# Power tables with the exponent innermost, and the backward state-space and dW2 placed beside the last block's transforms

## The chip, the cores and the metric

The kernel runs on one core of one Trainium2 chip. The metric is the time of one execution on the device in microseconds; three executions of the kernel before gave 1028.64, 1029.13 and 1033.02 us, the median is 1029.13. A core has five engines with a queue of instructions each, served in order: PE (matrix products and transposes; PEld is its loading of weights), DVE (elementwise work), ACT (activation functions and copies), POOL and SP (here SP issues nearly all DMAs). [...]

## The reference

The program computes a forward pass and all gradients of it. With x of shape [2048, 512] and xn its layer norm without scale, s a long convolution whose kernel comes from a diagonal complex state space of 128 states for each of 512 channels, and an FFN with 1792 hidden units:

```python
    dt = exp(log_dt)[:, None];  logdA = dt * (A_re + 1j*A_im);  dB = dt * (B_re + 1j*B_im)
    P = exp(logdA[:, :, None] * l[None, None, :])            # l = 0 .. 2047
    K = einsum("dn,dnl,dn->dl", C_re + 1j*C_im, P, dB).real
    s = irfft(rfft(xn, padded) * rfft(K, padded)) + xn * Dskip
    g = silu(silu(xn @ w1) @ w2)
    out = x + s * g
```

Returned are `out` and the gradients with respect to x, the six state-space matrices, log_dt, Dskip, w1 and w2, for a given `grad_out`, all in bf16.

## The kernel before, in words

**Layout.** The 2048 positions are kept as 128 partitions by 16; the 512 channels are cut into four blocks of 128 (b = 0 to 3), the hidden units into 14 tiles of 128 (`ft`).

**Power tables.** The state-space kernel K needs exp(logdA * l) for l up to 2047. A power is put together as a product of a low and a high factor; the factors are tables of 64 channels ("a half", eight in all, built in turn into one buffer `T4`). `half_angles` (L448) multiplies lam by 24 exponents into `PC` (magnitudes `MG`, cosines and sines `RC`, f32) and takes Exp and Sin on ACT; `half_tables` (L466) multiplies magnitudes and cosines into the bf16 tables. `PC` is laid out as [3, 24 exponents, 64 channels], so the channel is innermost in all that is read and written there; the tables `vXL` and `vYL` (L471, L473) are laid out with the exponent innermost in memory and are viewed here with the channel innermost, so that the 448-element multiplies of L484 and L486 write every eighth bf16 element. `vXH` (L490) writes runs of fourteen. L495 to L501 make the factors Fc and G (f32, 3 exponents); ACT copies them into `vYH`.

**Forward state-space** (`gen_ssm_fwd`, a generator of 106 steps): per group of channels DVE multiplies table factors into `X` and `ym`, PE transposes them (the results go to DRAM as `xt_d` and `yt_d` for the backward pass) and sums K, which goes to `K_b` of its block.

**Convolution.** `gen_conv_y(b)` (30 steps) transforms xn and K of one block (`dft_fwd`: two sets of products with a set of transposes between them), multiplies (`cplx_mul`, on DVE) and transforms back (`dft_inv`) to s; it also makes DO, the gradient at the FFN's output, and the output block. `gen_conv_rest(b)` (29 steps) transforms the gradient ds and gives the gradient of xn (`DXC`) and of K (`dKs`), with two inverse transforms. Every product of these lands in PSUM and is evacuated by `k.ev`, an `Evac` object (L63): `Evac(nc, 0)` gives all copies to ACT, `Evac(nc, 2)` (`k.ev2`) every second one to DVE.

**Backward.** `gen_ffn_bwd`, three steps for each `ft`: the hidden activations `a_ft` and `th_ft` are loaded, `turn` transposes `a_ft` (16 transposes on PE, two evacuations); `da` = 16 products with W2T and DOT; DVE makes `dhT`; dW2 = 16 products of the turned activations with `DO_all`; then `dhT` is turned and dW1 = 16 products with xn, turned and stored. `gen_ssm_bwd(b)` (25 steps): for eight groups of channels products `psV` (8 matmuls) with `Gbd` (made from dKs), evacuation to `Vb`, multiplies with `YT` on DVE, and sums `psS` (8 matmuls). `gen_ssm_final`, for blocks 0 to 2 and then for block 3, turns the sums into gradients on DVE with many small DMAs. `gen_dx`: 16 groups of 14 products with dhT and W1T, then the layer norm's gradient on DVE and ACT.

**Order.** The program is written as generators whose steps are merged by `interleave` with weights. Order by hand, L206 to L245: FFN forward beside 42 steps of the forward state-space; y and rest of blocks 0 and 1 beside 26 steps each; y of block 2 beside the last 12; then, alone, y of block 3 (in a second set of buffers, `C3`), rest of block 2, `load_bwd` (W2T, DO_all and DOT by DMA, the first and last transposing), rest of block 3; then FFN backward beside 110 steps of backward state-space and finals, one to three; then dx. The framework lays each engine's instructions out in about this order; an instruction that by its own estimate isn't ready lets later, ready ones pass, and it inserts all waits.

**Memory.** Pools are stacks from the left and from the right of a partition's memory, the right one ending at byte 229344; constants fill the left up to byte 37024. A pool opened where another was waits, tile by tile, for the last user of what lay there.

Of the kernel before, what the change touches and what calls it, by code (L numbers as in the profile page):

```python
# [14 lines left out]
P = 128  # L15
# [12 lines left out]
T = 16  # L28
# [123 lines left out]
def kernel(ctx, tc, A_u, A_A_re, A_A_im, A_B_re, A_B_im, A_C_re, A_C_im, A_log_dt, A_Dskip, B_x, B_w1, B_w2, grad_out,  # L152
# [35 lines left out]
    k.ev = Evac(nc, 0); k.ev2 = Evac(nc, 2)  # L188

    st_l = ExitStack(); st_tf = ExitStack()  # L190
    k.tfp = st_tf.enter_context(pool("tf", "left"))
# [9 lines left out]
    k.K_b = {}  # L201
    gs = gen_ssm_fwd(k)
# [6 lines left out]
    st_c = ExitStack(); st_c3 = ExitStack(); st_f = ExitStack()  # L209
# [9 lines left out]

    C3 = KCtx(); C3.big = st_c3.enter_context(pool("cbig3", "left")); C3.io = st_c3.enter_context(pool("cio3", "left"))  # L220
    run(gen_conv_y(k, C3, NB - 1))
    run(gen_conv_rest(k, C, NB - 2))
    st_c.close()
    k.e1 = ctx.enter_context(pool("keep", "right"))
    k.fb = st_f.enter_context(pool("ffnb", "right"))
    load_bwd(k)
    run(gen_conv_rest(k, C3, NB - 1))
    st_c3.close(); st_tf.close()
    dhp = ctx.enter_context(pool("dhT", "left"))
    k.dhT = dhp.tile([P, k.FT, L], BF16, name="dhT")  # L230
    def state():
        with pool("ssmb", "left", 2) as k.bp:
            k.Gbd = k.bp.tile([P, 2, 2, 32, 64], BF16, name="Gbd", bufs=1)
            for e in range(2):
                nc.gpsimd.memset(k.Gbd[64 * e:64 * e + 64, :, 1 - e], 0.0)
            for b in range(NB):
                yield from gen_ssm_bwd(k, b)
# [4 lines left out]
    interleave([gen_ffn_bwd(k), BoundedGen(gst, 110)], [1, 3])  # L242
# [205 lines left out]
def half_angles(k, w0):  # L448
# [6 lines left out]
    sh = [P, 2, 24, 64]  # L455
    tmul(nc, PC[:, 0:3:2], k.lam[:, 0:2, ws].unsqueeze(2).to_broadcast(sh), k.ecst[:].rearrange("p (a m) -> p a m", a=2).unsqueeze(3).to_broadcast(sh))
# [5 lines left out]
    nc.scalar.activation(out=RC[:, 1, 0:10], in_=RC[:, 1, 0:10], func=ACT.Sin, scale=2.0 * math.pi)  # L462
    nc.scalar.activation(out=RC[:, 1, 10:24], in_=RC[:, 1, 10:24], func=ACT.Sin, scale=-2.0 * math.pi)


def half_tables(k, w0):  # L466
# [4 lines left out]
    vXL = T4[:, OXL:OXH].rearrange("p (c r l) -> p c l r", c=3, l=8)  # L471
    vXH = T4[:, OXH:OYL].rearrange("p (c r l u) -> p c r l u", c=2, l=8, u=2)
    vYL = T4[:, OYL:OYH].rearrange("p (c g y r l) -> p c l g y r", c=2, y=2, r=4, l=8)  # L473
    vYH = T4[:, OYH:HSZ].rearrange("p (c g y r m u) -> p c g y r m u", c=2, y=2, r=4, m=4, u=2)
    if w0 == 0:
        for c in range(3):
            nc.gpsimd.memset(vXL[:, c, 0], 1.0 if c == 0 else 0.0)
        for c in range(2):
            v = 1.0 - c
            nc.gpsimd.memset(vXH[:, c, :, 0, :], v)  # L480
            nc.gpsimd.memset(vYL[:, c, 0, :, 0, :], v)
            nc.gpsimd.memset(vYH[:, c, :, 0, :, 0, :], v)
    for c in range(2):
# [3 lines left out]
    nc.vector.tensor_scalar(out=T4[:, OXL + 1024:OXH], in0=T4[:, OXL + 512:OXL + 1024], scalar1=-1.0, scalar2=None, op0=ALU.mult)  # L487
    for c in range(2):
        hh = lambda t: t[:, 17:24].rearrange("p m r -> p r m").unsqueeze(3).to_broadcast([P, 64, 7, 2])
        tmul(nc, vXH[:, c, :, 1:8, :], hh(MG), hh(RC[:, c]))  # L490
    yl = T4[:, OYL:OYH].rearrange("p (a y r) -> p a y r", y=2, r=32)
    nc.vector.tensor_copy(out=yl[:, :, 1], in_=yl[:, :, 0])
    sh = [P, 2, 3, 64]
    Fc = RC[:, :, 7:10]
    tmul(nc, Fc, MG[:, 7:10].unsqueeze(1).to_broadcast(sh), Fc)  # L495
# [441 lines left out]
```

## Time and profile before

| | us |
|---|---|
| median of three executions | 1029.13 |
| profiled execution | 1028.81 |
| its span, first to last instruction | 1027.0 |
| PE, DVE, ACT busy in it | 761.4, 746.6, 649.1 |

A row of the profile's groups gives line, engine, operation, the tile written and those read, the shapes, the count, then the busy time in us and the mean of one in ns, and what ended the idle time before. L60, L72 and L74 are helpers (`tmul`, the two copies of `Evac`), so their groups are told apart by tile names. In rows of the timeline the first number is the start in us from the span's begin, the second the length.

### The profile page before, as it was taken

What the parts mean: (1) busy time and instruction counts of PE and PEld (TensorE: products, weight loads), DVE (VectorE), ACT (ScalarE), POOL (GpSimd) and SP (SyncE); (2) the same over time, 40 slices, a digit from 0 to 9 for tenths busy, and PEclk for the clock granted to TensorE, in tenths of its full rate; (3) what the DMA queues carried; (4) which work ended last, traced back from release to release, by engine and by line L of the source; (5) the groups of instructions that cost most, each with busy time, mean ns of one, the idle gap of its engine ahead of it and who ended that gap; (6) DMA issues with size and microseconds to landing.
All of it is one profiled execution on the core that took longest, in us unless ns stands there. A gap on an engine that the chain in (4) does not pass through costs nothing. (4 is left out here: it accounts for less than half of the span.)

```text
span 1027.0 us, 17231 instructions
## 1 busy us (share of the span) xinstructions
PE 761.4 (74%) x6809; PEld 480.1 (47%) x6809; DVE 746.6 (73%) x1191; ACT 649.1 (63%) x1122; POOL 21.3 (2%) x86
## 2 busy tenths in 40 slices
PE   0276868888766667666777677699889998996693
PEld 0144545454646556465655455444445444443241
DVE  6997979899789995899805363646567755586497
ACT  1677696988969878697777777544545553442022
POOL 3100000000000000000000002000000000000000
PEclk9778989999988978889888888899999999999897
DMA  5054465746754444253759119976688877648771
GB/s 118 12 193 154 165 190 170 201 153 201 175 54 119 109 103 63 41 137 97 122 108 81 15 42 212 245 200 215 172 259 232 244 182 222 202 130 108 82 139 50
DMA packets 218034, 146.76 MB, mean 143 GB/s; under 512 B 155424, under 2 KB 187552, under 8 KB 217952
## 3 DMA queue, kind: packets, MB, share of 16 engines
q1 hardware_dynamic: 216608, 139.89, 56.4%
q0 software_dynamic: 768, 3.67, 1.0%
q10 hardware_dynamic: 576, 2.10, 0.6%
q8 instruction: 53, 0.87, 0.4%
q14 instruction: 29, 0.24, 0.1%
HBM read 74.84 MB, written 62.13 MB: 133 GB/s over the span
## 5 line engine op out<-in xcount | busy, mean ns | idle before, releaser
L540 PE MATMUL pf_t<-ident_bfloat_78,X 128*128 128x128 bf16 x1024 | 79.4, 232 | 46.6 <-ACT th L601 12.2
L74 ACT CAST Vb<-psV 128x512 bf16<-128x512 f32 x128 | 66.9, 603 | 69.6 <-issue 45.5
L514 DVE TENSOR_TENSOR ym<-T_512 128x1024 bf16<-128x1024 bf16 x128 | 83.3, 690 | 27.8 <-PE pf_y L557 26.2
L540 PEld LDWEIGHTS <-X 128*128 128x128 bf16 x1024 | 69.2, 105 | 56.3 <-issue 38.9
L514 DVE TENSOR_TENSOR X<-T_512 128x1024 bf16<-128x1024 bf16 x128 | 81.8, 690 | 9.9 <-remote 5.8
L60 DVE TENSOR_TENSOR T_512<-PC 128x448 bf16<-128x448 f32 (+1 forms) x48 | 84.0, 1872 | 0.4 <-ACT PC L461 0.4
L74 ACT CAST XTf<-pf_t 128x512 bf16<-128x512 f32 x128 | 66.9, 631 | 0.3 <-PE pf_t L540 0.3
L611 PE MATMUL ps_o<-W_412,aT 128*128 128x512 bf16 x224 | 55.6, 405 | 12.4 <-ACT th_1502 L615 6.6
L769 PE MATMUL ps_dx<-W1T,dhT 128*128 128x512 bf16 x224 | 53.3, 404 | 14.3 <-DVE dxn L772 8.9
L597 PE MATMUL ps_h<-XNT,W_410 128*128 128x512 bf16 x224 | 55.3, 392 | 7.6 <-ACT th L601 7.6
L74 ACT COPY dftB<-pt_b 128x1024 bf16<-128x1024 bf16 x48 | 46.9, 1026 | 14.5 <-remote 7.3
L726 PE MATMUL ps_da<-DOT,W2T 128*128 128x512 bf16 x224 | 53.4, 379 | 0.2 <-ACT dKs L74 0.2
L808 PE MATMUL psV<-XT,Gbd 128*128 128x256 bf16 x256 | 39.5, 284 | 8.9 <-DMA XT<-xt_d 5.7
L95 PE MATMUL pt_b<-ident_bfloat_78,dftA 128*128 128x128 bf16 x384 | 35.3, 254 | 12.2 <-ACT dftA L74 8.4
L769 PEld LDWEIGHTS <-dhT 128*128 128x128 bf16 x224 | 23.0, 103 | 44.3 <-issue 21.0
L808 PEld LDWEIGHTS <-Gbd 128*128 128x128 bf16 x256 | 32.5, 176 | 19.9 <-issue 15.6
L739 PEld LDWEIGHTS <-DH 128*128 128x128 bf16 x224 | 20.1, 98 | 45.3 <-ACT DH L74 19.0
L611 PEld LDWEIGHTS <-aT 128*128 128x128 bf16 x224 | 22.5, 103 | 39.5 <-issue 19.1
L87 PEld LDWEIGHTS <-TF 128*128 128x128 bf16 x384 | 28.4, 108 | 25.0 <-issue 24.1
L778 ACT ACTIVATE lw<-xn,mm 128x512 f32<-128x512 bf16 x16 | 13.0, 813 | 42.8 <-DVE mm L775 40.6
L727 DVE SCALAR_TENSOR_TENSOR dhT<-th_ft,ps_da 128x512 bf16<-128x512 bf16 x56 | 35.6, 680 | 5.7 <-PE ps_da L726 5.5
L557 PE MATMUL pf_y<-ident_bfloat_78,ym 128*128 128x128 bf16 x384 | 38.9, 234 | 0.2
(1477 smaller groups left out, 1952.7 us busy)
## 6 DMA issues: line engine op xcount, KB each, us to landing
xt_d<-XTf SPq DMA_DIRECT2D x32, 512.0 KB, 2.9
XT<-xt_d SPq DMA_DIRECT2D x32, 512.0 KB, 4.6
YT<-yt_d SPq DMA_DIRECT2D x64, 256.0 KB, 4.1
yt_d<-YTf SPq DMA_DIRECT2D x32, 256.0 KB, 2.1
th_d<-th SPq DMA_DIRECT2D x28, 256.0 KB, 2.3
at_d<-aT SPq DMA_DIRECT2D x4, 1792.0 KB, 6.8
a_ft<-at_d SPq DMA_DIRECT2D x14, 512.0 KB, 4.8
th_ft<-th_d SPq DMA_DIRECT2D x14, 512.0 KB, 5.7
```

The source lines that it names most:

```text
L60: nc.vector.tensor_tensor(out=out, in0=a, in1=b, op=ALU.mult)
L74: self.nc.scalar.copy(out=out, in_=in_)
L95: nc.tensor.transpose(out=pt[:, gi, :], in_=A[:, c, g0 + gi, :, :].rearrange("p t e -> p (t e)"), identity=k.ident[:])
L514: nc.vector.tensor_tensor(out=out.rearrange("p (r h l u) -> p r h l u", h=nh, l=4, u=2), in0=h, in1=l, op=ALU.mult)
L540: nc.tensor.matmul(out=pf[:, qi, m // 2, :], lhsT=X[:, m, q + qi], rhs=k.ident[:], start=(m % 2 == 0), stop=(m % 2 == 1))
L557: nc.tensor.matmul(out=pt[:, Qi, m // 2, :], lhsT=ms[m][:, Q + Qi, 0], rhs=(k.nident if m == 1 else k.ident)[:], start=(m % 2 == 0), stop= ...
L597: nc.tensor.matmul(out=ps[:], lhsT=W1[:, dk, ft * P:(ft + 1) * P], rhs=XNT[:, dk, 4 * tcn:4 * tcn + 4, :], start=(dk == 0), stop=(dk == DK ...
L611: nc.tensor.matmul(out=pso[:], lhsT=aT[:, ft, tt * P:(tt + 1) * P], rhs=W2[:, ft, :], start=(ft == 0), stop=(ft == FT - 1))
L726: nc.tensor.matmul(out=ps[:], lhsT=k.W2T[:, dk, rows], rhs=k.DOT[:, dk, ls], start=(dk == 0), stop=(dk == DK - 1))
L727: nc.vector.scalar_tensor_tensor(out=k.dhT[:, ft, ls], in0=th[:, ls], scalar=1.0, in1=ps[:], op0=ALU.add, op1=ALU.mult)
L769: nc.tensor.matmul(out=ps[:], lhsT=k.dhT[:, ft, t * P:(t + 1) * P], rhs=W1T[:, ft, :], start=(ft == 0), stop=(ft == FT - 1))
L808: nc.tensor.matmul(out=psV[:, qi].rearrange("p a b -> p (a b)"), lhsT=Gbd[:, :, :, :, 32 * (q_ // 2 % 2) + 4 * c + 2 * (q_ % 2) + q_ // 4] ...
```

## The change

**Tables.** `PC` becomes [3, 64 channels, 24 exponents]; the multiplies into vXL, vYL and vXH read and write with the exponent innermost (runs of seven), and those of vXL for both parts are one instruction. Fc, g1, g2 and G are then rows of three exponents out of 24.

**Order.** Blocks 0 to 2 get y and rest beside the forward state-space, all in one set of buffers (`C`); then ten steps of y of block 3 (its xn transform), the end of the state-space, and the other twenty steps with `k.ev2`. DO of blocks 0 to 2 is loaded into `DO_all` before that, block 3 writes its part there itself. Then rest of block 3, thirty steps of the backward state-space and dW2 (now a loop of its own, `gen_dw2`, which loads and turns the activations itself) are merged three to two to one. After it `gen_dh` does da, dhT and dW1, two steps for each `ft`, beside 80 steps of the state-space and finals, with W2T and DOT loaded at its beginning and W1T after its second `ft`; then dx.

**Smaller edits.** S_b, DXC and dKs take dftB's buffer; `ym` has seven buffers in place of six; TF, TI and K_b lie on the right; the evacuations of dW1 and dW2 and of Vb are `k.ev0` (ACT); the stores of dW1, dW2 and the state-space sums go to POOL's queue.

```diff
-    for b in range(NB - 2):
+    for b in range(NB - 1):
         upto(b)
         interleave([BoundedGen(gs, 26), chain([gen_conv_y(k, C, b), gen_conv_rest(k, C, b)])], [1, 2])
-    upto(NB - 2)
-    interleave([BoundedGen(gs, 26), gen_conv_y(k, C, NB - 2)], [1, 1])
+    last = gen_conv_y(k, C, NB - 1)
+    for _ in range(10):
+        next(last)
     upto(NB - 1)
     run(gs)
     st_l.close()
...
-    run(gen_conv_y(k, C3, NB - 1))
-    run(gen_conv_rest(k, C, NB - 2))
-    st_c.close()
...
-    run(gen_conv_rest(k, C3, NB - 1))
...
+    k.DO_all = k.e1.tile([P, T, D], BF16, name="DO_all", tag="big")
+    nc.sync.dma_start(k.DO_all[:, :, 0:(NB - 1) * P], dov[:, :, 0:(NB - 1) * P])
+    k.ev = k.ev2
+    run(last)
...
-    interleave([gen_ffn_bwd(k), BoundedGen(gst, 110)], [1, 3])
+    next(gst)
+    def dw2():
+        yield from gen_dw2(k)
+        st_1.close()
+    gd = dw2()
+    interleave([gen_conv_rest(k, C, NB - 1), BoundedGen(gst, 30), gd], [3, 2, 1])
+    st_c.close(); st_tf.close()
+    dhp = ctx.enter_context(pool("dhT", "right"))
+    k.dhT = dhp.tile([P, k.FT, L], BF16, name="dhT")
+    k.fb = st_f.enter_context(pool("ffnb", "right"))
+    interleave([gen_dh(k), BoundedGen(gst, 80)], [1, 3])
...
-    PC = sp.tile([P, 3, 24, 64], F32, name="PC", tag="PC", bufs=1)
+    PC = sp.tile([P, 3, 64, 24], F32, name="PC", tag="PC", bufs=1)
...
-    for c in range(2):
-        tmul(nc, vXL[:, c, 1:8], MG[:, 10:17], RC[:, c, 10:17])
-        g4 = lambda t: t[:, 0:7].rearrange("p m (g r) -> p m g r", r=4)
-        tmul(nc, vYL[:, c, 1:8, :, 0, :], g4(MG), g4(RC[:, c]))
...
+    tmul(nc, vXL[:, 0:2, :, 1:8], two(MG[:, :, 10:17]), RC[:, :, :, 10:17])
...
+        g4 = lambda t: t[:, :, 0:7].rearrange("p (g r) m -> p g r m", r=4)
+        tmul(nc, vYL[:, c, :, 0, :, 1:8], g4(MG), g4(RC[:, c]))
...
-    S_b = C.io.tile([P, T, P], BF16, name="S_b", tag="S_b")
+    S_b = C.big.tile([P, T, P], BF16, name="S_b", tag="dftB", padded_shape=[P, 2 * T, P])
...
+def gen_dw2(k):
+    nc, psum, c1 = k.nc, k.psum, k.c1
+    D, FT = k.D, k.FT
+    o11v = k.outs[11].rearrange("(k p) d -> p k d", p=P)
+    for ft in range(FT):
+        a = c1.tile([P, 2048], BF16, name="a2", tag="a2", bufs=2)
+        nc.sync.dma_start(a[:], k.at_d[ft * P:(ft + 1) * P, :])
+        A_ft = turn(k, c1, a, "A_ft")
+        ps = psum.tile([P, D], F32, name="ps_w2", tag="ps")
+        for t in range(T):
+            nc.tensor.matmul(out=ps[:], lhsT=A_ft[:, t, :], rhs=k.DO_all[:, t, :], start=(t == 0), stop=(t == T - 1))
+        ob = c1.tile([P, D], BF16, name="o11b", tag="ob", bufs=2)
+        k.ev0(ob[:], ps[:])
+        nc.gpsimd.dma_start(o11v[:, ft, :], ob[:])
+        yield
+
+
+def gen_dh(k):
...
+    W2T = fb.tile([P, DK, F], BF16, name="W2T")
+    nc.sync.dma_start_transpose(out=W2T[:], in_=k.ins["B_w2"])
+    DOT = fb.tile([P, DK, 2048], BF16, name="DOT")
+    nc.sync.dma_start_transpose(out=DOT[:], in_=k.do_d[:].rearrange("t p d -> (t p) d"))
...
+        if ft == 1:
+            k.W1T = k.e1.tile([P, T, D], BF16, name="W1T", tag="big")
+            nc.sync.dma_start_transpose(out=k.W1T[:, 0:FT, :], in_=k.ins["B_w1"])
```

More of the change, by code (lines that the diff above doesn't have):

```diff
@@ L201 @@
     k.K_b = {}
+    k.DO_all = None
     gs = gen_ssm_fwd(k)
@@ L670, in gen_conv_rest @@
     yield
-    DXC = C.io.tile([P, T, P], BF16, name="DXC", tag="S_b")
+    DXC = C.big.tile([P, T, P], BF16, name="DXC", tag="dftB", padded_shape=[P, 2 * T, P])
     yield from dft_inv(k, C, KX[:], DXC, k.ev)
@@ L675, in gen_conv_rest @@
     yield
-    dKs = C.io.tile([P, T, P], BF16, name="dKs", tag="S_b")
+    dKs = C.big.tile([P, T, P], BF16, name="dKs", tag="dftB", padded_shape=[P, 2 * T, P])
     yield from dft_inv(k, C, UX[:], dKs, k.ev)
@@ L725, in gen_ffn_bwd @@
             for dk in range(DK):
-                nc.tensor.matmul(out=ps[:], lhsT=k.W2T[:, dk, rows], rhs=k.DOT[:, dk, ls], start=(dk == 0), stop=(dk == DK - 1))
+                nc.tensor.matmul(out=ps[:], lhsT=W2T[:, dk, rows], rhs=DOT[:, dk, ls], start=(dk == 0), stop=(dk == DK - 1))
             nc.vector.scalar_tensor_tensor(out=k.dhT[:, ft, ls], in0=th[:, ls], scalar=1.0, in1=ps[:], op0=ALU.add, op1=ALU.mult)
         yield
-        ps = psum.tile([P, D], F32, name="ps_w2", tag="ps")
-        for t in range(T):
-            nc.tensor.matmul(out=ps[:], lhsT=A_ft[:, t, :], rhs=k.DO_all[:, t, :], start=(t == 0), stop=(t == T - 1))
-        ob2 = fb.tile([P, D], BF16, name="o11b", tag="ob", bufs=2)
-        k.ev2(ob2[:], ps[:])
-        nc.sync.dma_start(o11v[:, ft, :], ob2[:])
-        yield
-        DH = turn(k.dhT[:, ft], "DH")
+        DH = turn(k, fb, k.dhT[:, ft], "DH")
         ps = psum.tile([P, D], F32, name="ps_w1", tag="ps")
@@ L756, in gen_dx @@
     xn, rstd = k.xn, k.rstd
[L757 to L758 removed]
+    W1T = k.W1T
     for t0 in range(0, T, 4):
```

104 lines of the change are left out of this document (42 added, 62 removed).

## The prediction

> **What bounds the kernel now.** I read the stage table first, because the busy shares of the page are means over stages with different limits.
>
> ```profile
> PE 761.4 (74%) x6809; PEld 480.1 (47%) x6809; DVE 746.6 (73%) x1191; ACT 649.1 (63%) x1122; POOL 21.3 (2%) x86
> ```
>
> Columns of the next view: stretch, its length, busy time of PE, PEld, DVE, ACT, POOL, granted clock, DMA share, GB/s.
>
> ```profile
> 53.00:265.00 212.00, 168.29 (x1606) 103.66 (x1603) 185.78 (x279) 172.21 (x315) 0.03 (x1) 0.92 0.55 177
> 265.00:505.00 240.00, 169.17 (x2179) 139.08 (x2177) 210.61 (x302) 194.82 (x356) 0.00 (x0) 0.88 0.47 101
> 505.00:624.00 119.00, 87.70 (x878) 64.31 (x878) 49.93 (x72) 89.20 (x160) 0.00 (x0) 0.86 0.51 67
> 624.00:656.00 32.00, 23.58 (x201) 16.00 (x200) 14.62 (x20) 23.66 (x43) 7.01 (x2) 0.89 1.16 240
> 656.00:941.00 285.00, 252.90 (x1675) 128.60 (x1672) 188.78 (x248) 133.61 (x212) 0.00 (x0) 0.98 0.71 201
> 941.00:973.00 32.00, 17.75 (x75) 7.59 (x75) 8.89 (x36) 1.40 (x4) 0.00 (x0) 0.83 0.99 85
> 973.00:1027.00 54.00, 36.00 (x154) 15.59 (x153) 46.23 (x118) 13.01 (x16) 0.00 (x0) 0.82 0.44 104
> ```
>
> From 53 to 505 (FFN forward, then blocks 0 and 1 of the convolution, both beside the forward state-space) DVE is busy 88% of the time, ACT 81%. From 505 to 656 the transforms run nearly alone: ACT 75%, DVE 43%. From 656 to 941 (FFN backward beside the backward state-space) PE is busy 89% at a clock of 0.98. After 941 DVE limits, once it starts at 973. Inside these first stages DVE is full where the tables are built; one such stretch, in the same columns:
>
> ```profile
> 105.00:125.00 20.00, 15.75 (x150) 9.40 (x149) 20.00 (x30) 12.19 (x27) 0.00 (x0) 1.00 0.40 131
> ```
>
> **Part 1, the tables.** Groups by shape; after the bar total and mean of one in ns.
>
> ```profile
> L60 DVE TENSOR_TENSOR T_512<-PC 128x448 bf16<-128x448 f32 x32 | 67.3, 2179 | 0.4 <-ACT PC L461 0.4
> L60 DVE TENSOR_TENSOR T_512<-PC 128x896 bf16<-128x896 f32 x16 | 20.0, 1257 | 0.0
> L60 DVE TENSOR_TENSOR PC<-PC,lam 128x384 f32<-128x384 f32 x16 | 8.4, 565 | 0.0
> L500 DVE TENSOR_TENSOR PC<-PC 128x192 f32<-128x192 f32 x8 | 2.9, 364 | 0.0
> ```
>
> From 192 to 384 elements a multiply grows by 201 ns: 1.05 ns an element and 163 ns fixed. The 448-element multiplies (vXL, vYL) should cost 0.63 us and take 2.18, which is 4.5 ns an element: each element is written 16 bytes from the one before. vXH writes runs of 14 elements and stays at 1257, close to 163 + 896 x 1.05 = 1104; the 153 ns over it, on 128 runs of 16 bytes, are 1.2 ns for each. The new layout writes vXL and vYL in runs of seven that fill one 16-byte row each. With 1.2 to 3.5 ns (4.5 - 1.05) for a new row, vXL in one instruction of 896 elements and 128 rows costs 1.26 to 1.55, each vYL (64 rows) 0.71 to 0.86; I take 1.4 and 0.78. Removed per half: 4 x 2.18 = 8.72; put in: 1.4 + 2 x 0.78 = 2.96; gain 5.8. vXH and the angle multiply keep their counts and their contiguous writes: 0. ACT's Sin now runs over rows of 10 and 14; 128 more rows at up to 3.5 ns are 0.45 per half at most, on the engine that has room there: 0.
>
> Against it stand three 384- and two 192-element f32 multiplies (Fc, g1, g2, G), whose rows of 64 become runs of three 24 words apart. If each run costs 1.2 to 3.5 ns once or twice, a 384-element one (128 runs) goes up by 0.15 to 0.9, a 192-element one by half of that; I take 0.4 and 0.2: 1.6 per half (0.6 to 3.6). Net 4.2 per half (2.0 to 5.7 with the bounds above), 34 us of DVE over eight halves. [...]
>
> How much reaches the end: in the table stretch DVE has no idle time and ACT has 39%, so the saving shortens them directly, until ACT (81%) is the next bound. Seven of eight halves lie in such stretches, the first beside the start. I take 70%: **24 us** (8 to 38).
>
> **Part 2, before the last block's transforms.** The order y2, y3, rest 2 becomes y2, rest 2, y3, the same evacuations; the last 20 steps of y3 now give every second one to DVE. Evacuations follow each other every 0.48 us, the bf16 ones of 1024 take about 1:
>
> ```profile
> 654.11 0.59 ACT L74 CAST dKs<-ps_i_8200 128x512 bf16<-128x512 f32 x1
> 654.59 0.60 ACT L74 CAST dKs<-ps_i_8210 128x512 bf16<-128x512 f32 x1
> ...
> 656.47 1.93 ACT L74 COPY A_ft<-pt_f 128x1024 bf16<-128x1024 bf16 x2 [0.79 <-PE pt_f L709]
> ```
>
> Those 20 steps hold 24 of the first kind on ACT (four more are DVE's already) and 4 of the second: 24 x 0.48 + 4 = 15.5; half of it, less DVE's slower copies, saves 6. One context in place of two, and S_b, DXC, dKs now in dftB's only buffer, cost up to 4 (a store has to land first). New is that state-space steps of block 0 may fill the gaps from the end of the tables on, because their memory is no longer the second context's; the framework does move ready work that far:
>
> ```profile
> L660 PE MATMUL ps_dsk<-xn,cat_b x64: 218/219/230, 268.1 to 543.3; 128*128 128x128 bf16 x64
> ```
>
> These are the Dskip products of all four rests (sixteen matmuls each); the last began at 543.3, though rest 3 has its place from 624 on. Three state-space groups at 2 us of PE (priced in part 3): 6, more only if ACT's gaps allow, since each also needs four evacuations. Together **8 us** gained (-8 to 20).
>
> **Part 3, rest 3, dW2 and the state-space together, then dh.** The pieces on PE, from one period of the old loop:
>
> ```profile
> 758.14 3.61 PE L731 MATMUL ps_w_9227<-DO_all,A_ft 128*128 128x512 bf16 x16
> ...
> 765.81 3.63 PE L739 MATMUL ps_w_9303<-xn,DH 128*128 128x512 bf16 x16 [1.78 <-ACT DH L74]
> ...
> 770.33 0.39 PE L746 MATMUL pt_w<-ident_bfloat_78,wt 128*128 128x128 bf16 x4
> ...
> 771.14 1.06 PE L709 MATMUL pt_f<-ident_bfloat_78,a_ft 128*128 128x128 bf16 x16
> ```
>
> One ft: three products of 3.62 (da has 16 matmuls of the same shape), two turns of 1.06, 0.39: 13.4, fourteen times 187. The rest of the 252.9 belongs to 32 state-space groups: 2.05 each. New first stretch: 23.6 (rest 3) + 14 x (3.61 + 1.06) + 10 groups x 2.05 (30 steps) = 109.5. dW2's matmuls now follow their turn in the same step, as dW1's did, and that has a price:
>
> ```profile
> PEld L739 <- ACT DH L74: 19.0, 12, 2.2
> ```
>
> 1.6 us each, so 0 to 22 for fourteen; conv steps stand ready to fill them: 11. Stretch 120.5. Second stretch: 14 x (3.62 + 1.06 + 3.63 + 0.39) + 22 x 2.05 = 167, DH stalls 19.0, and of the other 13 idle (285 - 252.9 - 19.0) about two thirds: 9; 195. Between them the new wait. dhT and ffnb are stacked down from byte 229344: 57344 and 59392 of them put W2T, ffnb's first tile, at 112608, below the 123040 where the w2 pool ends (37024 + 16384 + 51200 + 18432). So W2T waits for the last dW2, and da(0) for W2T, whose like took:
>
> ```profile
> 624.30 9.08 SPq L687 DMA_TRANSPOSE W2T<-in_B_w_dram  x1
> ...
> 935.85 6.99 SPq L758 DMA_TRANSPOSE W1T<-in_B_w_dram  x1
> ```
>
> ```profile
> L694 SPq DMA_TRANSPOSE DOT<-do_d x4: 2090/3477/5048, 633.5 to 643.9; - x4
> ...
> DMA to landing us min/median/max: 5.9/6.2/6.5
> ```
>
> In before rest 3 covered this. W1T, of W2T's size, landed 11.7 after its start (PE's row below), so some 14 for W2T; four state-space groups fill 8, since XT and YT loads stand behind it on SP: 6 to 7 lost, 0 to 36 as bounds (nothing, or SP's 9.1 for W2T, 4 x 3.5 for DOT, 6 to land, W1T's 7). Sum 120.5 + 195 + 6.5 = 322 against 32 + 285 = 317: **5 us** lost (12 gained to 45 lost). At nothing I cost: the second load of at_d, 14 x 512 KB, 60 GB/s over the first stretch, where 201 were moved from 656 to 941; the stores of s_d, o11b and o10b on GpSimd's queue, for which no engine waits but W2T once; the 21 evacuations of o11b, wt and o10b that go from DVE to ACT (0.6 each; ACT has 151 us free from 656 to 941); the move of the TF pool and the seventh ym buffer. If ACT had no room, those 21 would cost 13. DO of the last block is written in place instead of by a load, so that dW2 can begin as soon as y3 ends.
>
> **Part 4, dx.** W1T now comes in dh. Before, it and the loads behind it held the stage:
>
> ```profile
> 942.93 0.53 SPq L907 DMA_DIRECT2D out_dram<-ddt_b_10880  x1
> ...
> 959.09 0.33 SPq L842 DMA_DIRECT2D n_Ci_10897<-in_A_C_im_dram  x1
> ...
> 968.46 0.42 SPq L761 DMA_DIRECT2D DXC_s<-dxc_d  x1
> ```
>
> ```profile
> 947.54 17.31 PE L769 MATMUL ps_dx<-W1T,dhT 128*128 128x512 bf16 x70 [5.42 <-DMA W1T<-in_B_w_dram]
> 973.71 6.65 PE L769 MATMUL ps_dx<-W1T,dhT 128*128 128x512 bf16 x18 [8.86 <-DVE dxn L772]
> ```
>
> n_Ci is the eighth transfer behind the scattered ddt_b and left 16 us after it; DXC_s was queued behind that, and DVE had 8.9 us of work in 32. With DXC_s early the stage is 54 of dx, 9 of the second final, about 10 of the first (the state-space now ends nearer to dx), 4 for the first product: 77, against 86. But SP can stall as before: 86, or 8 more. I take **8 us** gained.
>
> Sum, against the profiled execution's own 1028.8 (span 1027.0 and 1.8 around it; the median of the runs is 0.3 above): 1028.8 - 24 - 8 + 5 - 8 = **994**.
>
> **Rivals.** (a) Only the tables pay: PE bounds the end at the same work, and dx keeps its stalls: 1028.8 - 24 = 1005. For it: 89% PE at 0.98; against it: 14 us of waits of PE in dx. (b) All of it hides: tables 34, gaps filled 15, dW2's stalls and W2T's wait gone (+12), dx 13: 955. For it: ACT has a quarter of 505 to 656 free; against it: W2T's place. (c) Slower, by SP's queue at the start of dh: W2T cannot start before the last dW2, DOT and W1T are issued around it, and XT, YT, a_ft, th_ft queue behind, so that PE stands for 36 us, with dW2's stalls in full (22): 109.5 + 22 + 195 + 36 = 362, 45 lost, and with 24 for the tables and 8 in part 2, but nothing in dx, 1042. It decides from a loss of 32 in part 3, where those 24 + 8 are used up. Against it: DOT has memory of its own earlier. (d) The tables do not get cheaper, since every run pays as much as an element did: the reordering alone, 1028.8 - 11 = 1018.
>
> **Numbers.** The forecast 46%, (a) 22, (b) 14, (c) 12, (d) 6. Range 952 to 1036, from (b) to just short of (c); around the forecast alone 976 to 1012. About 0.5%, 5 us, is what a measurement tells from no change here. Faster by more: the forecast, (a), (b) and part of (d), 0.81; within: 0.07; slower: 0.12.
>
> **What would show it.** The 896-element vXL near 1.4 us and 448 near 0.8; the 384-element f32 ones near 0.95; table stretches with DVE no longer full. The DVE-poor stretch, 151 us in the stage table, down to about 110; PE idle of 1 to 2 us ahead of dW2's matmuls, one gap near 7 us ahead of the first da, and ps_dx starting right after the last dW1. A gap above 30 us there, or vXL above 3 us, makes the forecast wrong.

## The result, and the profile after

The changed kernel took 998.65 us (median of 995.93, 996.19, 1001.12 and 1005.68); the kernel before, in four executions, 1031.08. The ratio is 0.9687, with a 95% interval of 0.9615 to 0.9759: some 32 us less. The forecast was 994, some 5 us under the median. Its parts did not come out as well as its sum, and that is what the rest is about.

The profiled execution of the changed kernel is the slowest of its four (1005.68, span 1003.9), 7 us above the median, so the stages below are a little long. First its busy times, to be set against 761.4, 746.6 and 649.1 before:

```profile
PE 740.6 (74%) x6809; PEld 470.2 (47%) x6809; DVE 709.8 (71%) x1198; ACT 640.3 (64%) x1107; POOL 36.8 (4%) x111
```

Then its stages. Columns: stretch, length, busy time of PE, PEld, DVE, ACT, POOL, granted clock, DMA share, GB/s. They are FFN forward; the convolution of blocks 0 to 2 beside the forward state-space; rest 2 and the last twenty steps of y3; rest 3 with dW2; the junction to the first da; dh; dx.

```profile
53.00:252.00 199.00, 166.94 (x1602) 105.23 (x1602) 164.26 (x276) 173.53 (x317) 0.61 (x1) 0.90 0.61 193
252.00:509.00 257.00, 186.81 (x2529) 152.60 (x2527) 200.98 (x318) 221.18 (x405) 7.01 (x2) 0.91 0.49 101
509.00:602.50 93.50, 58.75 (x558) 42.16 (x559) 45.25 (x66) 55.43 (x99) 0.00 (x0) 0.84 0.67 111
602.50:712.00 109.50, 93.86 (x754) 55.78 (x754) 53.49 (x73) 61.70 (x95) 7.60 (x14) 1.00 0.63 182
712.00:737.70 25.70, 3.37 (x18) 1.35 (x17) 2.43 (x3) 2.54 (x5) 0.54 (x1) 0.58 1.10 235
737.70:924.30 186.60, 171.97 (x1077) 85.45 (x1078) 138.83 (x170) 90.26 (x149) 6.62 (x9) 0.98 0.76 223
924.30:1003.90 79.60, 53.71 (x229) 23.11 (x227) 62.86 (x177) 15.04 (x22) 0.75 (x1) 0.84 0.53 98
```

The forward state-space ends at 509; before it was 531. Its last copy, of KF, in the kernel before and in the changed one (count, duration in ns, first and last start):

```profile
L74 ACT CAST KF<-ps_k x64: 357/368/486, 78.9 to 531.4; 64x256 bf16<-64x256 f32 x64
L74 ACT CAST KF<-ps_k x64: 347/367/503, 74.2 to 509.2; 64x256 bf16<-64x256 f32 x64
```

From there to the end of rest 2 and y3 both kernels need 93 us, although the new order has less left to do there. The kernel before, in the columns of the stage table, has 70 us of ACT's work where the changed one has 55:

```profile
531.40:624.00 92.60, 68.53 (x602) 48.35 (x600) 41.59 (x57) 70.22 (x123) 0.00 (x0) 0.85 0.48 62
```

Rest 3, dW2, the junction and dh take 321.8 (109.5 + 25.7 + 186.6), where the stages that answer to them took 317. The last stage, counted from the end of dh, went from 86 (941 to 1027) to 82 (922 to 1004), or to 79.6 from the first product of dx as in the table.

The table multiplies, in the groups by shape (busy us, mean ns):

```profile
L60 DVE TENSOR_TENSOR T_512<-PC 128x896 bf16<-128x896 f32 x24 | 25.4, 1087 | 0.4 <-ACT PC L469 0.4
...
L60 DVE TENSOR_TENSOR T_512<-PC 128x448 bf16<-128x448 f32 x16 | 10.0, 623 | 0.1
L60 DVE TENSOR_TENSOR PC<-PC,lam 128x384 f32<-128x384 f32 x16 | 9.2, 613 | 0.0
...
L60 DVE TENSOR_TENSOR PC<-PC 128x384 f32<-128x384 f32 x8 | 4.9, 614 | 2.4 <-ACT PC L470 2.4
...
L508 DVE TENSOR_TENSOR PC<-PC 128x192 f32<-128x192 f32 x8 | 3.1, 393 | 0.1
```

The multiplies into T_512 went from 87.3 us (67.3 + 20.0) to 35.4; those on runs of three hardly rose, from 565 and 364 ns to 613 and 393.

The waits of the changed kernel that stand out (who, for whom: total us, times, longest):

```profile
PE pt_b L95 <- ACT dftB L74: 15.9, 2, 15.2
ACT dftB L74 <- DMA dk_d<-dKs: 14.8, 1, 14.8
...
PEld L712 <- ACT A_ft L74: 17.1, 13, 2.0
...
PE ps_da L740 <- DMA DOT<-do_d: 19.3, 1, 19.3
...
DVE n_ndt_11074 L858 <- ACT n_dtb_11072 L856: 10.0, 1, 10.0
```

In order: the shared buffer of dftB (two rows), the turns ahead of dW2's products, the junction, and the second final, whose first DVE step is queued ahead of dx's. SyncE's queue at the first, at the junction and in the second final (start, length):

```profile
545.05 2.35 SPq L676 DMA_DIRECT2D out_dram<-ddb  x1
...
550.42 0.32 SPq L687 DMA_DIRECT2D dk_d<-dKs  x1
...
712.30 7.73 SPq L759 DMA_TRANSPOSE W1T<-in_B_w_dram  x1
720.38 7.19 SPq L725 DMA_TRANSPOSE W2T<-in_B_w_dram  x1
727.62 7.93 SPq L727 DMA_TRANSPOSE DOT<-do_d  x1
...
940.97 0.39 SPq L916 DMA_DIRECT2D out_dram<-ddt_b_11051  x1
...
945.09 0.43 SPq L851 DMA_DIRECT2D n_Ci_11068<-in_A_C_im_dram  x1
955.93 0.33 SPq L854 DMA_DIRECT2D n_ldt_11070<-in_A_log_dt_dram  x1
```

The store of dKs, of rest 2, stands 5 us behind the store of ddb, and ACT gets dftB only at 569.1, 18.7 us after it was issued. This ddb belongs to rest 3 already: its Dskip products, which the framework had moved ahead, ended at 540. At the junction W1T, last of the three in the program, is issued first and holds the other two back. And behind ddt_b, a store of 384 single elements of two bytes (those of the convolution, ddb, have 128), the queue stops for 11 us. What the DMA engines do meanwhile, in the columns of the stage table:

```profile
941.00:957.00 16.00, 13.86 (x65) 6.17 (x63) 7.63 (x19) 1.74 (x3) 0.00 (x0) 1.00 0.98 29
```

They are busy at 0.98 and move 29 GB/s.

### The profile page after: what moved, and what is told of

The parts are those of the page before. It is cut to its first block, busy times and chain, and to the rows that moved or that the text cites. A ratio compares the mean times of both kernels' runs of the same rounds, so it can differ in the third digit from the quotient of the medians.

```text
span 1003.9 us, 17264 instructions
## 1 busy us (share of the span) xinstructions
PE 740.6 (74%) x6809; PEld 470.2 (47%) x6809; DVE 709.8 (71%) x1198; ACT 640.3 (64%) x1107; POOL 36.8 (4%) x111
## 5 line engine op out<-in xcount | busy, mean ns | idle before, releaser
L548 PEld LDWEIGHTS <-X 128*128 128x128 bf16 x1024 | 68.4, 104 | 44.6 <-issue 34.1
L740 PE MATMUL ps_da<-DOT,W2T 128*128 128x512 bf16 x224 | 54.3, 394 | 19.3 <-DMA DOT<-do_d 19.3
L74 ACT COPY dftB<-pt_b 128x1024 bf16<-128x1024 bf16 x44 | 42.4, 1031 | 20.1 <-DMA dk_d<-dKs 14.8
L95 PE MATMUL pt_b<-ident_bfloat_78,dftA 128*128 128x128 bf16 x384 | 30.4, 232 | 23.9 <-ACT dftB L74 19.0
L740 PEld LDWEIGHTS <-W2T 128*128 128x128 bf16 x224 | 22.4, 101 | 46.5 <-issue 25.3
L572 PE MATMUL ps_k<-GG,X 128*128 128x64 bf16 x1024 | 36.9, 196 | 5.0 <-issue 4.5
L572 PEld LDWEIGHTS <-X 128*128 128x128 bf16 x1024 | 35.6, 100 | 10.6 <-issue 6.3
L712 PEld LDWEIGHTS <-A_ft 128*128 128x128 bf16 x224 | 20.8, 98 | 40.6 <-ACT A_ft L74 17.1
```

The source lines that it names most:

```text
L74: self.nc.scalar.copy(out=out, in_=in_)
L95: nc.tensor.transpose(out=pt[:, gi, :], in_=A[:, c, g0 + gi, :, :].rearrange("p t e -> p (t e)"), identity=k.ident[:])
L548: nc.tensor.matmul(out=pf[:, qi, m // 2, :], lhsT=X[:, m, q + qi], rhs=k.ident[:], start=(m % 2 == 0), stop=(m % 2 == 1))
L572: nc.tensor.matmul(out=ps[:, q].rearrange("p e j -> p (e j)"), lhsT=X[:, m, q], rhs=GG[:, m // 2, q // 2, 64 * (q % 2):64 * (q % 2) + 64], ...
L740: nc.tensor.matmul(out=ps[:], lhsT=W2T[:, dk, rows], rhs=DOT[:, dk, ls], start=(dk == 0), stop=(dk == DK - 1))
```

## The experiments

Each result is given as a ratio to the kernel before on the same chip, since that kernel's median ranged from 1030.6 to 1036.4 us between the chips.

### The tables alone, the order alone

The kernel before with the new `half_angles` and `half_tables`:

```diff
-    PC = sp.tile([P, 3, 24, 64], F32, name="PC", tag="PC", bufs=1)
+    PC = sp.tile([P, 3, 64, 24], F32, name="PC", tag="PC", bufs=1)
...
-        tmul(nc, vXL[:, c, 1:8], MG[:, 10:17], RC[:, c, 10:17])
+    tmul(nc, vXL[:, 0:2, :, 1:8], two(MG[:, :, 10:17]), RC[:, :, :, 10:17])
```

> The kernel before with the new exponent-innermost tables and nothing else. Theory of the prediction (the saving of the tables is worth about 24 us by itself, because DVE is full where they are built): 1031 - 24 = 1007 us, forward state-space ending about 20 us sooner than 531, the rest of the trace shifted whole. Rival, the order pays: the trace of the changed kernel shows a saving of 50 us of DVE and an end of the state-space only 22 us sooner, in an order that also changed, so the tables alone could bring 10 or less (1021 or above). Rival, all of it pays: 87.3 to 35.4 us of DVE, 995 or less.

Measured: 1001.05 us, ratio 0.968 (0.9634 to 0.9726).

```profile
PE 751.0 (75%) x6809; PEld 472.9 (47%) x6809; DVE 702.4 (70%) x1183; ACT 647.0 (65%) x1122; POOL 21.3 (2%) x86
```

DVE has 44 us less to do, the time is 31 less, between the 24 of the theory and the 36 or more of "all of it". The last copy of KF stands at 494.3, 37 us sooner than in the kernel before, where the changed kernel has it 22 sooner: beside more transforms the state-space takes 15 us longer, by one trace each. The other half, the changed kernel with the old layout:

```diff
-    PC = sp.tile([P, 3, 64, 24], F32, name="PC", tag="PC", bufs=1)
+    PC = sp.tile([P, 3, 24, 64], F32, name="PC", tag="PC", bufs=1)
```

> The changed kernel with the old layout of the tables (exponent outermost); its order, pools and queues as changed. Theory: by the stages of the two profiles the order brings 0 in part 2, loses 3 in part 3 and gains 4 in dx, so about 1030 (1025 to 1034). Prediction as on record: 11 gained, about 1020. Rival, the two need each other: above 1036, since the state-space then ends at about 531 and the last block cannot begin sooner.

Measured: 1028.39 us, ratio 0.9964 (0.994 to 0.9988). The order brings 0.4%, with DVE's old load. Added to the tables (0.9687 against 0.968) it brings nothing that can be told. So the tables pay for nearly all of the 32 us, and the question is where the order's gain went.

### S_b, DXC and dKs off dftB's buffer

They take the buffers of operands that are dead by then, so that no memory is added.

```diff
-    S_b = C.big.tile([P, T, P], BF16, name="S_b", tag="dftB", padded_shape=[P, 2 * T, P])
+    S_b = C.big.tile([P, T, P], BF16, name="S_b", tag="PX", padded_shape=[P, 2 * T, P])
...
-    DXC = C.big.tile([P, T, P], BF16, name="DXC", tag="dftB", padded_shape=[P, 2 * T, P])
+    DXC = C.big.tile([P, T, P], BF16, name="DXC", tag="KX", padded_shape=[P, 2 * T, P])
...
-    dKs = C.big.tile([P, T, P], BF16, name="dKs", tag="dftB", padded_shape=[P, 2 * T, P])
+    dKs = C.big.tile([P, T, P], BF16, name="dKs", tag="PX", padded_shape=[P, 2 * T, P])
```

> The changed kernel with S_b, DXC and dKs in the buffers of YX, KX and YX (their own operands, dead by then) in place of dftB's. Theory: the 14.8 us in which ACT waits for the store of dKs before it writes dftB (and PE 15.2 with it) lie on the path; 998 - 13 = 985 (983 to 988). Rival, the time is given back at the next wait (cat_b and x_b of the last block, loaded behind the same scattered store of ddb, are late as well): less than 4 gained, 994 to 999.

Measured: 987.74 us, ratio 0.9543 (0.9484 to 0.9602), 1.4% of the kernel before under the changed kernel's 0.9687. In its trace the way from the last copy of KF to the end of y3 takes 77 us (514.4 to 591.6) in place of 93. The wait lay on the path.

### The scattered stores, from another queue and as rows

Two explanations of the late store of dKs and of the stop behind ddt_b were open: SyncE's queue, which stops some transfers later (in both second finals seen so far it is the eighth behind ddt_b that goes out late: n_Ci in the kernel before, 16.2 us after it, n_ldt in the changed one, 15.0 us after it), or the DMA engines themselves. First the two scattered stores on GpSimd's queue:

```diff
-        nc.sync.dma_start(k.outs[9][blk].rearrange("(p o) -> p o", o=1), ddb[:])
+        nc.gpsimd.dma_start(k.outs[9][blk].rearrange("(p o) -> p o", o=1), ddb[:])
...
-        nc.sync.dma_start(k.outs[8][bs].rearrange("(k p) -> p k", p=P), ddt_b[:])
+        nc.gpsimd.dma_start(k.outs[8][bs].rearrange("(k p) -> p k", p=P), ddt_b[:])
```

> The changed kernel with the two scattered stores of 2-byte elements, ddb (out 9) and ddt_b (out 8), issued from GpSimd's queue in place of SyncE's. Theory: n_ldt of the second final is the eighth transfer behind ddt_b on SyncE (945.1 to 955.9), DVE stands 10.0 us for it and the end moves by 8 to 10; and the store of dKs no longer lands late (14.8 of dftB's wait), so up to 13 more: 975 to 990. Rival, the scattered stores slow all transfers from any queue: both waits stay, 996 to 1000. Between: only dx pays, 989.

Measured: 1009.16 us, ratio 0.977 (0.9726 to 0.9813): nothing gained; the interval overlaps that of the changed kernel. Its queue of SyncE in dx:

```profile
945.89 0.43 SPq L854 DMA_DIRECT2D n_ldt<-in_A_log_dt_dram  x1
```

n_ldt is now issued at once, half a us behind n_Ci and 10 us sooner than in the changed kernel. It lands no sooner. The waits of the same place, and the DMA engines there:

```profile
ACT n_dtb L856 <- DMA n_ldt<-in_A_log_dt_dram: 14.9, 1, 14.9
...
DVE n_ndt L858 <- ACT n_dtb L856: 12.3, 1, 12.3
```

```profile
942.00:958.00 16.00, 13.16 (x61) 5.86 (x60) 7.79 (x21) 1.63 (x2) 0.32 (x1) 1.00 1.16 27
```

n_ldt needs 16.4 us from its issue; in the changed kernel, where it left after the stop, it was there in under 3 (955.93 to the ACT step at 958.72). The queue only showed the stop: with the store issued by GpSimd the DMA engines are no less busy (1.16 against 0.98) and move no more (27 GB/s against 29).

Then the same outputs as rows. A product with the identity turns the column into a row on PE, and the store is one run:

```diff
+def as_rows(k, pool, col, n):
+    ps = k.psum1.tile([P, P], F32, name="ps_row", tag="psd")
+    k.nc.tensor.matmul(out=ps[0:n, :], lhsT=col[:], rhs=k.ident[:], start=True, stop=True)
+    row = pool.tile([n, P], BF16, name="row%d" % n, tag="row")
+    k.nc.vector.tensor_copy(out=row[:], in_=ps[0:n, :])
+    return row
...
-        nc.sync.dma_start(k.outs[9][blk].rearrange("(p o) -> p o", o=1), ddb[:])
+        nc.sync.dma_start(k.outs[9][blk].rearrange("(o p) -> o p", o=1), as_rows(k, C.io, ddb, 1)[:])
...
-        nc.sync.dma_start(k.outs[8][bs].rearrange("(k p) -> p k", p=P), ddt_b[:])
+        nc.sync.dma_start(k.outs[8][bs].rearrange("(k p) -> k p", p=P), as_rows(k, fin, ddt_b, DK)[:])
```

> The changed kernel with outs 8 and 9 stored as rows: a product with the identity turns the column of 128 values into one row (exact in bf16), so that the store is one run of 256 bytes in place of 128 elements of 2 bytes. Theory: the scattered stores hold the transfer engines (DMA share 0.98 at 29 GB/s for the 16 us behind ddt_b), whatever queue they come from, so dftB's wait of 14.8 and DVE's 10.0 in dx both go: 999 - 13 - 9 = 977 (972 to 984). Rival, the eighth-transfer wait of SyncE's queue is the cause: the same gain would have come from GpSimd's queue, which took 1009; then nothing here, 997 to 1009. Rival, only dx pays: 990.

Measured: 956.32 us, ratio 0.9212 (0.9158 to 0.9265), 4.8% or some 48 us under the changed kernel: twice what was expected. Its stages, in the order of the changed kernel's from rest 2 on:

```profile
488.00:562.50 74.50, 55.69 (x547) 40.98 (x548) 42.65 (x64) 54.32 (x95) 0.00 (x0) 0.91 0.59 138
562.50:673.00 110.50, 93.42 (x749) 56.60 (x761) 54.07 (x73) 62.35 (x97) 7.61 (x14) 1.00 0.62 180
673.00:698.70 25.70, 2.76 (x15) 0.96 (x13) 2.43 (x3) 2.49 (x5) 0.54 (x1) 0.59 1.10 238
698.70:885.20 186.50, 170.05 (x1059) 85.33 (x1078) 138.61 (x170) 90.27 (x149) 6.63 (x9) 0.97 0.76 223
885.20:954.00 68.80, 49.32 (x227) 21.91 (x229) 63.11 (x179) 14.96 (x22) 0.75 (x1) 0.90 0.38 113
```

No stop is left: n_Ci and n_ldt go out at 906.44 and 906.91. The last copy of KF stands at 486.1. Of the 50 us between the two spans, 23 lie ahead of that (486.1 against 509.2: there the stores of ddb run beside the forward state-space), 17 from there to the end of y3 (93.3 to 76.4), 11 in dx (79.6 to 68.8); the three stages between have not moved. The expectation had 13 and 9 for the last two and had left out the first.

The same edit on the kernel before with the new tables, in the old order, shows what the order is worth with these stores out of the way:

> The kernel before with the new tables and with outs 8 and 9 stored as rows, its order as it was. Beside the run with rows on the changed kernel (956) it shows what the order is worth without the scattered stores. Theory: in the new order one of these stores falls just ahead of the store of dKs for which dftB waits (14.8), in the old order no such wait stands, so the rows bring less here, about 32 (two stores beside the state-space 20, dx 11): 1001 - 32 = 969, and the order's own worth is then 12. Rival, the rows bring the same 45 in both: 956, the order is worth 2 to 3 either way. Rival, the order pays all of it: above 980.

Measured: 968.66 us, ratio 0.9379 (0.9327 to 0.9431). So the rows bring 3.0% in the old order and 4.8% in the new, and the order's own worth is 0.9379 against 0.9212: 1.7%, some 17 us. That is the gain that did not show in the changed kernel. In the old order the last copy of KF stands at 476.5, and from there to the end of rest 2 it takes as long as before:

```profile
476.50:571.40 94.90, 70.72 (x602) 49.36 (x600) 42.24 (x59) 70.20 (x123) 0.00 (x0) 0.82 0.33 61
```

The new order needs 76.4 for the way that answers to it, but its state-space ends 10 us later, so that these transforms end 9 us sooner (562.5 against 571.4). Dx is 2 shorter (71.0 to 68.8) and the rest 1, which makes the 12 between the two spans (966.2 and 954.2).

### The junction

W2T goes into memory of its own at the left and is loaded ahead of the last twenty steps of y3; o11b gives up a buffer and Ss takes T1's slot to make room; DOT lies above the w2 pool; W1T is issued behind DOT.

```diff
-    W2T = fb.tile([P, DK, F], BF16, name="W2T")
-    nc.sync.dma_start_transpose(out=W2T[:], in_=k.ins["B_w2"])
+    W2T = k.W2T
...
-            nc.sync.dma_start_transpose(out=k.W1T[:, 0:FT, :], in_=k.ins["B_w1"])
+            with k.tc.issue_after(dot.ins): nc.sync.dma_start_transpose(out=k.W1T[:, 0:FT, :], in_=k.ins["B_w1"])
...
-    Ss = bp.tile([P, 512], F32, name="Ss", tag="Ss", bufs=1)
+    Ss = bp.tile([P, QCH * P], F32, name="Ss", tag="T1", bufs=1)[:, 0:512]
```

> The changed kernel with W2T in memory of its own (pool keep; o11b with one buffer, Ss in T1's slot), loaded before the last block, DOT above the w2 pool, and W1T issued behind DOT. Theory: of the 19.3 us that PE stands before the first da, W1T's 7.7 and W2T's 7.2 on SyncE's queue go, DOT's 7.9 and its landing stay with some state-space work to cover: a gap of 4 to 10, 999 - 12 = 987 (984 to 991). Prediction's step (W2T alone costs 6 to 7): 992. Rival, a transposing load costs the same wherever it stands, since the state-space loads are queued behind it: 996 to 1002.

Measured: 1004.0 us, ratio 0.968 (0.9619 to 0.9741), no change. Groups by tile, and two stretches (end of dW2 to the first da; dh):

```profile
L740 PE MATMUL ps_da<-DOT,W2T 128*128 128x512 bf16 x217 | 52.8, 393 | 6.8 <-DMA DOT<-do_d 6.5
```

```profile
711.00:725.00 14.00, 4.45 (x22) 1.86 (x21) 2.43 (x3) 2.54 (x5) 0.54 (x1) 0.68 0.93 213
725.00:922.00 197.00, 173.92 (x1059) 87.32 (x1076) 138.71 (x171) 91.18 (x149) 6.26 (x9) 0.96 0.77 217
```

The gap shrank as the theory had it, from 19.3 to 6.5 us, but dh took 197 us in place of 186.6 and gave 10 of the 13 back. Part of that was probably my own squeeze of Ss; the last runs below bear on it.

### Turning ahead of the products

In dW2 the turn of the next ft stands ahead of this one's products; in dh, da of the next ft stands between turn and dW1.

```diff
-    for ft in range(FT):
+    def load(ft):
...
-        A_ft = turn(k, c1, a, "A_ft")
+        return turn(k, c1, a, "A_ft")
+    nxt = load(0)
+    for ft in range(FT):
+        A_ft, nxt = nxt, (load(ft + 1) if ft + 1 < FT else None)
...
+    da(0)
+    for ft in range(FT):
         DH = turn(k, fb, k.dhT[:, ft], "DH")
+        if ft + 1 < FT:
+            da(ft + 1)
+        yield
```

> The changed kernel with the turn of the next ft ahead of the products of this one, in dW2 and in dh (there da of the next ft also stands between turn and product). Theory: the stalls before dW2's products (17.1 us in all) and before dW1's (12.4) go, since PE is busy 95 of 111 and 169 of 184 us there: 999 - 22 = 977 (972 to 985). Rival, the conv and state-space steps that fill PE are bound by ACT's copies, and the turn's copies only move in their queue: 10 or less gained, 989 or above. Prediction's step: dW2's stalls cost 11 of a possible 22.

Measured: 991.76 us, ratio 0.9544 (0.9455 to 0.9633), 1.4% under the changed kernel, though the two intervals just overlap. The stages from rest 3 to dh:

```profile
600.00:692.00 92.00, 90.80 (x733) 55.61 (x746) 53.06 (x72) 60.41 (x94) 7.60 (x14) 1.00 0.75 211
692.00:718.00 26.00, 2.81 (x11) 0.69 (x11) 2.43 (x3) 1.79 (x4) 0.54 (x1) 0.56 1.13 241
718.00:912.00 194.00, 174.40 (x1059) 86.11 (x1074) 137.20 (x167) 89.24 (x147) 6.59 (x9) 0.94 0.73 213
```

dW2's stretch went from 109.5 to 92 us with PE busy for 90.8 of them, so dW2's stalls were worth 17, all that the waits showed. dh became 7 longer, although DH's stalls went too. Its clock was 0.94 in place of 0.98, and PE's busy time per matmul rose by 3% (174.40 / 1059 against 171.97 / 1077), which would be some 5 us of the 7 (an estimate from these two rows). Neither theory had that; the later runs turn only dW2 around.

### State-space steps written into y3

```diff
-    run(last)
...
-    next(gst)
+    next(gst); interleave([last, BoundedGen(gst, 12)], [2, 1])
...
-    interleave([gen_dh(k), BoundedGen(gst, 80)], [1, 3])
+    interleave([gen_dh(k), BoundedGen(gst, 68)], [1, 3])
```

> The changed kernel with 12 steps (4 groups) of the backward state-space of block 0 written between the last 20 steps of y3 and 12 fewer behind dh. Theory: in the changed kernel nothing of it moved into y3's gaps by itself (the first psV stands at 601.6 though its Gbd was there from 512), because its PSUM tiles come from the ring that the transforms use, in program order; written there, 4 x 2.05 us of PE leave the full stretches: 999 - 6 = 993 (989 to 996). Rival, y3 lasts as much longer as the groups take, four copies of ACT each at 0.6: 998 to 1004.

Measured: 1004.64 us, ratio 0.9684 (0.9623 to 0.9744), no change. The evacuations of psV, and the stretch of dW2:

```profile
L74 ACT CAST Vb<-psV x128: 585/605/765, 560.6 to 871.9; 128x512 bf16<-128x512 f32 x128
```

```profile
592.00:713.00 121.00, 98.49 (x779) 59.35 (x791) 55.17 (x78) 63.18 (x98) 7.61 (x14) 0.97 0.71 172
```

The first group now stands at 560, in the gaps, and y3 even ended 12 us sooner (590.4 against 602.6, 4 of it from ahead of the stage), since in this order dftB did not meet the late store. But the stretch of dW2 took 121 us in place of 109.5 and ended where it had. One reason is in SyncE's queue: rest 3 kept its place here, so that its scattered store of ddb now falls into this stretch, and a load of at_d stands right behind it.

```profile
641.37 0.34 SPq L675 DMA_DIRECT2D out_dram<-ddb  x1
641.80 0.38 SPq L707 DMA_DIRECT2D a<-at_d  x1
```

```profile
PE pt_f L696 <- DMA a<-at_d: 5.3, 1, 5.3
```

PE gets this load at 661.3, 19.5 us after its issue, and the next load of at_d leaves the queue only at 662.3. So the cost of the store was moved, not saved, and what the groups in the gaps are worth by themselves these runs don't show. The rest of the 11.5 us stays open.

### Together

Rows, the buffers of S_b, DXC and dKs, and dW2 turned around:

> The changed kernel with rows for outs 8 and 9, S_b, DXC and dKs in YX's and KX's buffers, and the turn of the next ft ahead of dW2's products. Theory: dW2's stretch goes from 111 to 92 us as in the run where both loops were turned around, and dh gives 5 to 8 of that back at a lower granted clock (0.94 in place of 0.98 there); the buffers bring 0 to 4 since no store lands late any more: 956 - 13 = 943 (939 to 949). Rival, all is given back by the clock: 953 to 957.

Measured: 937.04 us, ratio 0.9059 (0.9007 to 0.9112), a little below the range, since dh gave nothing back: 185 us at a clock of 0.98. With the junction as above:

> The kernel of the run before (rows, buffers, dW2 turned around) with W2T in memory of its own and loaded early, DOT above the w2 pool, W1T behind DOT. Theory: PE's gap before the first da goes from 19 to 7, but the granted clock and psV's waits give it back in dh, as they did alone: within 4 us of the run before, 939 to 947. Rival, the give-back was chance of that order: 12 less, 931.

Measured: 936.49 us, ratio 0.9062 (0.9019 to 0.9106). As alone, the junction brought nothing. Its trace held a wait that the kernel without it has not:

```profile
DVE T L60 <- DMA s_d<-Ss: 5.1, 1, 5.1
```

So the last run moved Ss:

```diff
-    Ss = bp.tile([P, QCH * P], F32, name="Ss", tag="T1", bufs=1)[:, 0:512]
+    Ss = bp.tile([P, QCH * P], F32, name="Ss", tag="Vb")[:, 0:512]
```

> The run before with one change: Ss takes a slot of Vb's two in place of T1's only one. Theory: what dh gave back after the shorter gap came from my own squeeze, since the first product into T1 of the next block waits until the store of Ss has landed (5.1 us in one place), and the steps around a change of block take 18.5 and 17.6 us in place of 14.6 and 13.0; with Vb that goes: 936 - 8 = 928 (924 to 932). Rival, the granted clock and psV's waits take back what the gap no longer costs, whatever Ss does: 933 to 939.

Measured: 931.81 us, ratio 0.903 (0.899 to 0.9069). The stretch up to the first da and dh in the last three kernels, one fence each:

```profile
656.00:682.00 26.00, 3.56 (x18) 1.41 (x17) 2.43 (x3) 2.54 (x5) 0.54 (x1) 0.57 1.10 241
682.00:867.00 185.00, 170.40 (x1072) 84.82 (x1071) 137.74 (x168) 89.81 (x148) 6.62 (x9) 0.98 0.76 223
```

```profile
656.00:669.00 13.00, 3.23 (x15) 0.98 (x14) 2.43 (x3) 2.54 (x5) 0.54 (x1) 0.69 1.03 230
669.00:864.00 195.00, 173.99 (x1072) 86.54 (x1071) 137.73 (x168) 90.56 (x148) 6.17 (x9) 0.97 0.77 219
```

```profile
651.00:664.00 13.00, 6.79 (x37) 2.89 (x32) 2.43 (x3) 3.13 (x6) 1.08 (x2) 0.89 0.84 199
664.00:857.00 193.00, 169.77 (x1070) 84.56 (x1071) 137.36 (x168) 90.50 (x148) 6.17 (x9) 0.98 0.80 227
```

From the first da (681.7, 668.6 and 667.5) to the first product of dx (868.0, 865.0 and 858.3), dh lasts 186, 196 and 191 us; dx takes 70 in all three. By these traces, one of each kernel, Ss accounts for about 5 of the 10 that had been given back, at nearly the same clock (0.97 and 0.98). Of the other 5 the traces show that PE stood 9.2 us ahead of psV's products in the last kernel and 4.2 in the first; why stays open. The intervals of the three kernels overlap, so in time the step from 0.9062 to 0.903 is likely but not shown; all three are 9 to 10% under the kernel before and 6 to 7% under the changed one.

## Why the prediction was right, step by step

**Part 1, the tables: the direction right, the share nearly, the price too high.** The forecast took 1.4 us for vXL, 0.78 for vYL and 0.4 and 0.2 more for the multiplies on runs of three. They took 1.09 (the group holds vXL and vXH; its longest is 1.094), 0.62, and 0.05 and 0.03 more, all outside the bounds that were set, on the cheap side. The mis-sized term is the price of a new row, 1.2 to 3.5 ns: 896 elements at 1.05 plus 163 are 1104 ns, and vXL took 1087, so here a new run of seven, in a row of 16 bytes, costs nothing, and one of three, 24 words apart, hardly anything (48 ns on 128 runs are 0.4 each). Where the 1.2 came from, vXH's excess over 1104, was no price of rows either: vXH is in the same group of 1087 now, written as before and only read in another order. Net, DVE saved 50 us on the tables (51.9 less 1.5 on the runs of three), not 34; alone they shortened the kernel by 31, 62% of it where 70% was taken. So 24 became 31. (The bounds of 2.0 to 5.7 per half, redone with the prediction's own numbers, are 1.9 to 5.4.) With all fixed cost, the 384-element multiplies on runs of three took 613 / 384 = 1.6 ns an element, where on rows of 64 they took 565 / 384 = 1.5.

**Part 2: 8 us forecast, 0 measured.** 93 us stand against 93, with 15 us of ACT's work moved ahead of them, where the state-space took as much longer. The sharing of dftB's buffer had been given up to 4; the wait was 14.8, and the buffers moved away brought 1.4%, some 15 us. The step that failed is "a store has to land first" priced as an ordinary store: this one was queued behind 128 single elements. And it was the very behaviour on which the prediction relied, ready work of rest 3 that moves far ahead, that put those elements in front of it. The other failed step is that the framework would move state-space groups into the gaps, 6 us: the first psV stood at 601.6, at the end of y3. The Dskip products, on which I rested that, have a PSUM bank outside the ring; psV shares a ring with the transforms. That this ring is the cause is argued, not shown. The trace has another bound too: the first load of XT went out only at 547.45 (and Gbd was complete from 523, not from 512 as a later expectation says), so psV could not have stood ahead of that whatever the ring did. Written into the gaps by hand, the groups ran there and the time stayed the same, but the scattered store had moved as well, so their worth is open. What the copies on DVE (`k.ev2`) are worth was not tried by itself. With the scattered stores gone the stage takes 76 where the old order takes 95; 10 of these 19 the state-space ahead gives back. The 9 that are left are close to the 8 of part 2, though no state-space groups are among them (the first psV of that run stands at 562.2).

**Part 3: 322 forecast, 321.8 measured, by errors that cancel.** The first stretch took 109.5, not 120.5: the work was 93.9 us of PE where 109.5 had been summed. dW2's products and turns came as summed (64.4 us in the stretch); the state-space took 16.3 in place of 20.5, since nine of ten groups fell into it; rest 3 leaves 13 of its 23.6. Those 23.6 held 2.5 us of the first da and a turn, they came from a stage at a clock of 0.89 where here it was 1.00, and some of rest 3 ran ahead of the stretch. The turn stalls were 17.1 where 11 was taken. All of these stalls lay on the path (109.5 to 92 when dW2 was turned around). The loop dh took 186.6, not 195. The junction took 25.7 with PE standing for 19.3, where 6 to 7 was forecast. The wait of W2T for dW2's end was seen rightly; that W1T would be issued ahead of it, 7.7 us on the queue, had only gone into the upper bound, and the four state-space groups that were to cover 8 us were queued behind the three transposing loads. Rival (c) had this mechanism at 36; it came at half of that.

**Part 4, dx: 8 forecast, 4 measured (6 from its first product on).** DXC_s was issued at 928.9 and ps_dx began at 924.3, right behind dh, as forecast. "SP can stall as before" came true: the second final's n_ldt was late by 11 us, and DVE, whose order has that final's steps between dx's, stood for 10. The mechanism in the prediction, the eighth transfer behind the scattered store, was wrong: that wait is there, but with the store in another queue the load lands just as late. With the outputs as rows, dx takes 68.8.

**The sum.** 24 + 8 - 5 + 8 = 35 forecast, 32 between the medians. With the tables at the 31 of their own run, the parts measured give 31 + 0 - 5 + 4 = 30. The two profiled executions alone give 22 ahead of 509, 0, -5 and 6, the 23 between their spans; the changed kernel's is its slowest. That the total came out is luck: the tables paid more than was taken and the order nothing, and the two errors cancel. In mechanism the result is nearest to rival (a), only the tables pay, with a larger price than the 24 which that rival had. The rival (d), tables that do not get cheaper, is refuted by the groups above; (b), all of it hides, did not come while the scattered stores stood.

## What to carry to other kernels

When a layout is changed for an engine, price it by its fixed cost and its rate on contiguous elements first: runs of seven in rows of 16 bytes cost no more here, single elements 16 bytes apart cost three and a half times as much (2179 against 623 ns). When an order is changed, ask what each shared buffer's last reader is: here a store of dKs that came 15 us late behind a scattered one of 128 elements cost 1.4%, by the run with the buffers moved, and the order by itself brought 0.4%. The busy times of the engines did not show it; the 16 us behind ddt_b, with a DMA share of 0.98 at 29 GB/s, did. And after a wait is removed, measure the stage behind it, with the same clock, before the gain is counted.

## What the runs showed of the hardware that was not expected

A store of 384 single two-byte elements held the DMA engines for about 16 us (share 0.98 and 1.16 at 29 and 27 GB/s), whichever of the two queues it was issued from; a load issued 4 us behind it landed 16.4 us after its issue. One of 128 made the store of dKs behind it 15 us late. Six such stores cost 48 us of the changed kernel and, by the run in the old order, some 31 of the other. A load of 128 scattered elements, with the store out of the way, was there in under 3 us.

PE's granted clock in dh was 0.94 in the one run that turned both loops around, behind a stretch with 90.8 busy us of 92, and 0.98 in the changed kernel, behind 93.9 of 109.5. A fuller stretch ahead does not explain it: in the first kernel of the last three that stretch had 91.7 busy us of 92, and dh kept 0.98. The cause stays open.
